# Where six chunks of x sums wait for their split, and which engine splits them

## The chip, the cores and the metric

The kernel runs on one core of a Trainium2 chip. The metric is the device time of one execution in microseconds (us), from the first to the last instruction and the little that lies around them; each version is run several times and the median counts. A core has a matrix engine (PE), a vector engine (DVE), an activation engine (ACT), GpSimd (POOL) and a sync engine (SP). Each takes its own instructions strictly in the order in which they were recorded. SP issues nearly all DMA transfers, ACT a few.

## What is computed

x has 2048 tokens of 576 features, all in float32:

```python
g = sigmoid((x * gate_w).sum(-1, keepdims=True))
a = linear_attention(x, wqkv, wo)                        # 32 heads of 18 features
b = (gelu(x @ w_gate) * (x @ w_up)) @ w_down             # 4608 hidden features
out = g * a + (1 - g) * b
```

## The kernel before

**Stages.** First come keys, values and their sums, then the queries and the attention's output, which is written to memory (`ga_d`) with the gate applied; then the gate and up products of `b`; then the down product, which adds all up. The change lies where the second stage ends and the third begins, between 260 and 310 us of the span.

**Numbers in two halves.** PE multiplies float32 in a rounded format (fp32r). So each operand is split: ACT copies it rounded into a high half, and DVE or POOL subtracts that copy from the raw value for the low half. One product of 128 x 512 results over half the features is then seven matmuls: six for the high and low halves of two blocks of 128 features, and one for the last 32 features.

**Gate and up.** A product of x and a weight block is done by Strassen's scheme: seven products of sums of blocks, numbered 1 to 7 in `PRODUCTS`, instead of eight. The seven operands that x gives are slots: `A11`, `A12` and `A22` (plain blocks) and the sums `S2`, `S4`, `S3`, `S1`. `xo` holds the seven slots of the first token half, `X[1]` (named `xo2` or `xo_3273`) those of the second. A weight block is loaded raw (`wraw`, in `stage`), POOL makes four differences of its blocks (`weight_sums`, L380), and `w_split` splits the seven operands into `W[GATE]` (`wg`) or `W[UP]` (`wu`): ACT L875, then POOL L876 and L877.

**Chains, frames, places.** One weight block on one token half is a chain of seven products; there are 72. A frame c has seven places i = 0 to 6: places 0, 4 and 5 run products 1, 6 and 2 of chain c, and places 1, 2, 3 and 6 run products 7, 5, 3 and 4 of chain c-1. Behind the product of a place, whatever `put` has entered in `plan[(frame, i)]` is recorded: loads, splits, sums, stores. Chain 0 is an exception: its first four products stand in the stage before, its fifth and sixth in frame 0, its seventh at place 1 of frame 1. Product 6 adds onto what product 1 left (a seed: ACT L948 or L950 copies one bank of results on; for the first chains DVE L956 then adds it), and products 2, 3 and 4 go on in the banks of 1, 6 and 7. So product 2 of chain 1 starts when ACT L948 has read the bank of product 1, and product 3 when another L948 has read the bank of product 6, once L956 has added to it. Product 4 follows DVE L983, which follows ACT L978 (the copy of product 5). DVE L922 and ACT L885 finish chain 0.

**The six chunks.** The sums S of the second token half are made early by POOL and stored to memory as `xsum_d[0..5]`, 512 KB each: chunk k has feature block k // 2 and 256 of the 512 token columns. `s_load(k)` (L1290, on SP) brings a chunk raw into one half of `f`, a buffer that later takes results of the second token half; `s_make(k)` splits it into `X[1]` (ACT L1295, then L1296, on DVE for chunks 0 to 3 and on POOL for 4 and 5). Chunks 0 and 1 are loaded ahead of frame 0 and chunk k + 2 right behind the split of k. The slots A11, A12 and A22 of `X[1]` are loaded ready-made from `xop_d` (L1363) at the places `X_AT`.

**Around it.** `w_fetch(1, 0)` (L865) loads the raw weights of chain 2, and L1324 those of chain 3. The last two stores of the attention's output (L797, issued by ACT from the buffer `ga`) are still under way here. `X[1]`, `f` and `stage` are new tiles which lie in memory that the stage before has used, so their first writer waits for the last user of what lay there.

Of the kernel before, what the change touches and what calls it, by code (L numbers as in the profile page):

```python
# [11 lines left out]
OP = mybir.AluOpType  # L12
# [102 lines left out]
A11, A12, A22, S2, S4, S3, S1 = range(7)  # L115
# [5 lines left out]
def tile_gated_mix(ctx, tc, xt, xs, xn, wk, wv, wq, wo, wgu, wdn, cst, out):  # L121
    nc = tc.nc
# [9 lines left out]
    xsum_d = [dram.tile([128, 4, 256], F32, name=f"xsum_d{k}") for k in range(6)]  # L132
# [8 lines left out]
    def f32(ap):  # L141
        return ap.bitcast(F32)
# [233 lines left out]
    def weight_sums(raw, out, parts=slice(0, 4)):  # L376
        b12, b11, b21, b22 = (raw[:, i] for i in range(4))
        t1, t2, t3, t4 = (out[:, i] for i in range(4))
        for o, a, b in ((t1, b12, b11), (t2, b22, t1), (t3, b22, b12), (t4, b21, t2))[parts]:
            nc.gpsimd.tensor_tensor(o, a, b, OP.subtract)  # L380
# [468 lines left out]
    X, ES = {0: xo}, {0: es}  # L849
# [14 lines left out]
    def w_fetch(n, m):  # L864
        nc.sync.dma_start(wraw, wgu[n, m])  # L865
        if (n, m) == (1, 1):
            nc.sync.dma_start(tsum, ws_d)
        else:
            weight_sums(wraw, tsum)
# [267 lines left out]
    f = stages.tile([128, 4, BS], F32, name="f")  # L1137
# [142 lines left out]
                h_load()  # L1280

    X_AT = {(0, 5): A11, (3, 4): A12, (4, 0): A22}
    S_AT = [(1, 1), (1, 4), (2, 1), (2, 5), (3, 1), (3, 3)]

    def s_raw(k):
        return f[:, k % 2 * 2:k % 2 * 2 + 2].rearrange("p a (b c) -> p (a b) c", b=2)

    def s_load(k):
        if k < 6:
            nc.sync.dma_start(s_raw(k), xsum_d[k])  # L1290

    def s_make(k):
        kt, c, raw = k // 2, slice(k % 2 * 256, k % 2 * 256 + 256), s_raw(k)
        rows, lo, eng = (slice(0, 128), 3 + kt, nc.vector) if kt < 2 else (slice(32, 64), kt, nc.gpsimd)
        nc.scalar.activation(X[1][:, S2:S1 + 1, kt, c], raw, AF.Copy)  # L1295
        eng.tensor_tensor(X[1][rows, S2:S1 + 1, lo, c], raw[rows], f32(X[1][rows, S2:S1 + 1, kt, c]), OP.subtract)  # L1296

    for k in range(2):
        s_load(k)
    w_fetch(1, 0)  # L1300
    LAST = len(CHAINS) - 1
    plan = {}

    def put(frame, i, do):
        plan.setdefault((frame, i), []).append(do)
# [45 lines left out]
    for g in range(NF2 // 2):  # L1351
        one = Sums(g)
        for at, what in one.tasks():
            frame, i = light[31 * g + at * 31 // 25]
            eng = nc.gpsimd if i > 3 or frame % 2 == 0 == i else nc.vector
            put(frame, i, lambda one=one, what=what, eng=eng: one.do(what, eng))
    for n, k in enumerate((1, 6, 2, 7, 5, 3, 4)):
        b = PRODUCTS[k][1]
# [2 lines left out]
            lambda b=b: nc.sync.dma_start(f32(last_up[:, b]), wp_d[1][:, b]))  # L1361
    for (frame, i), a in X_AT.items():
        put(frame, i, lambda a=a: nc.sync.dma_start(f32(X[1][:, a]), xop_d[:, a]))  # L1363
    for k, (frame, i) in enumerate(S_AT):
        put(frame, i, lambda k=k: s_make(k))
        put(frame, i, lambda k=k: s_load(k + 2))
    kept = [(0, es[1], (2, 4), (LAST, 1)), (1, sx[:, 0], (2, 4), (LAST, 1)), (2, es[2], (2, 6), (LAST, 3))]
    for c in range(1, LAST):
        for (frame, i), does in sorted(extras(c).items()):
            for do in does:  # L1370
                put(c + frame, i, do)
    late = extras(LAST)
    for do in late.pop(0):
        put(LAST, 4, do)
# [176 lines left out]
```

## Time and profile before

| | |
|---|---|
| median of 3 runs | 1445.23 us (1443.6 to 1445.69) |
| the profiled execution | 1443.79 us, span 1442.0 us, granted PE clock 1.000 |
| PE busy | 1435.1 us, in 8096 matmuls |
| DVE, ACT, POOL busy | 995.8, 640.5, 824.4 us |
| DMA | 312.69 MB, mean 217 GB/s |

In a timeline row stand the start and the length in us, the engine (SPq and ACTq are the issue of a DMA, not its transfer), the line of the code, the operation, output<-inputs, the shape, how many instructions the row merges, and in brackets how long the engine idled before it and what ended that. A matmul of a stream is shown with 0.39 us, though the next starts after 0.227 us: the ends are modelled and overlap. In a row of time windows stand the window, the busy us of each engine, the granted clock, the mean busy share of the 16 DMA engines and the GB/s (1 GB/s is 1 KB per us) that they moved.

### The profile page before, as it was taken

What the parts mean: (1) busy time and instruction counts of PE and PEld (TensorE: products, weight loads), DVE (VectorE), ACT (ScalarE), POOL (GpSimd) and SP (SyncE); (2) the same over time, 40 slices, a digit from 0 to 9 for tenths busy, and PEclk for the clock granted to TensorE, in tenths of its full rate; (3) what the DMA queues carried; (4) which work ended last, traced back from release to release, by engine and by line L of the source; (5) the groups of instructions that cost most, each with busy time, mean ns of one, the idle gap of its engine ahead of it and who ended that gap; (6) DMA issues with size and microseconds to landing.
All of it is one profiled execution on the core that took longest, in us unless ns stands there. A gap on an engine that the chain in (4) does not pass through costs nothing. (4 is left out here: it accounts for less than half of the span.)

```text
span 1442.0 us, 21510 instructions
## 1 busy us (share of the span) xinstructions
PE 1435.1 (100%) x8096; PEld 1281.3 (89%) x8096; DVE 995.8 (69%) x1139; ACT 640.5 (44%) x863; POOL 824.4 (57%) x541
## 2 busy tenths in 40 slices
PE   9999999999999999999999999999999999999999
PEld 9999899978888888888888888888889999999998
DVE  7887898355865648646485554766578777799793
ACT  7554656444333433334433344333355455444542
POOL 1674543366555655655556455564236565589895
PEclk9999999999999999999999999999999999999999
DMA  7573485774654556454664555655799989866761
GB/s 260 154 216 112 163 281 184 248 272 153 219 184 163 178 189 227 168 174 166 206 223 156 188 175 169 231 172 186 271 368 336 354 294 355 321 219 249 241 214 34
DMA packets 148552, 312.69 MB, mean 217 GB/s; under 512 B 14744, under 2 KB 61528, under 8 KB 147296
## 3 DMA queue, kind: packets, MB, share of 16 engines
q1 hardware_dynamic: 145856, 306.34, 62.1%
q10 hardware_dynamic: 2592, 4.98, 0.9%
q8 instruction: 63, 1.03, 0.3%
q14 instruction: 41, 0.34, 0.1%
HBM read 200.78 MB, written 110.44 MB: 216 GB/s over the span
## 5 line engine op out<-in xcount | busy, mean ns | idle before, releaser
L861 PE MATMUL bank<-xo,wg 128*128 128x512 f32 x1764 | 415.4, 389 | 0.3 <-ACT bank L950 0.2
L861 PE MATMUL bank<-xo,wu 128*128 128x512 f32 x1715 | 403.5, 389 | 0.3 <-ACT bank L950 0.3
L861 PEld LDWEIGHTS bank<-xo,wg 128*128 128x128 f32 x1764 | 330.9, 188 | 69.4 <-ACT bank L950 0.7
L861 PEld LDWEIGHTS bank<-xo,wu 128*128 128x128 f32 x1715 | 321.9, 188 | 67.5 <-ACT bank L950 0.8
L1437 PE MATMUL bank<-xo 128*128 128x288 f32 x2124 | 283.7, 294 | 0.7 <-DVE acc L1447 0.7
L1437 PEld LDWEIGHTS bank<-xo 128*128 128x128 f32 x2124 | 281.4, 188 | 1.1 <-DVE acc L1447 1.0
L380 POOL TENSOR_TENSOR stage<-stage 128x384 f32<-128x384 f32 x132 | 139.6, 1078 | 173.8 <-DMA stage<-wgu 144.0
L950 ACT ACTIVATE bank<-bank 128x512 f32<-128x512 f32 x139 | 80.9, 582 | 238.3 <-PE bank L861 230.1
L1240 POOL TENSOR_TENSOR xo<-vt,xo 128x864 fp32r<-128x864 f32 x39 | 112.7, 2892 | 51.5 <-ACT xo L1239 48.7
L1240 POOL TENSOR_TENSOR xo<-stage,xo 128x864 fp32r<-128x864 f32 x33 | 93.8, 2843 | 82.9 <-ACT xo L1239 57.0
L876 POOL TENSOR_TENSOR wg<-stage,wg 128x768 fp32r<-128x768 f32 (+3 forms) x41 | 73.8, 1801 | 87.9 <-ACT wg L875 84.1
L983 DVE TENSOR_TENSOR bank<-bank,mid 128x512 f32<-128x512 f32 x36 | 25.1, 697 | 133.4 <-ACT mid L978 133.4
L876 POOL TENSOR_TENSOR wu<-stage,wu 128x768 fp32r<-128x768 f32 (+2 forms) x36 | 75.1, 2087 | 62.6 <-ACT wu L875 56.3
L1437 PE MATMUL bank<-xo,wu 128*128 128x288 f32 x684 | 93.3, 294 | 0.0
L1437 PEld LDWEIGHTS bank<-xo,wu 128*128 128x128 f32 x684 | 91.3, 188 | 0.0
L978 ACT ACTIVATE mid<-bank 128x512 f32<-128x512 f32 x71 | 42.4, 597 | 102.2 <-PE bank L861 94.0
L980 DVE TENSOR_TENSOR f<-bank,mid 128x512 f32<-128x512 f32 x18 | 12.4, 692 | 96.8 <-ACT mid L978 93.0
L788 PEld LDWEIGHTS pair<-kw,p 128*128 128x128 f32 x448 | 60.8, 189 | 1.0
L788 PE MATMUL pair<-kw,p 128*128 128x288 f32 x448 | 61.4, 295 | 0.0
L538 PE MATMUL bank<-xo,qw 128*128 128x512 f32 (+1 forms) x231 | 55.7, 392 | 0.0
L538 PEld LDWEIGHTS bank<-xo,qw 128*128 128x128 f32 (+1 forms) x231 | 41.9, 183 | 10.0
L313 POOL TENSOR_TENSOR psum_k<-psum_k,e 128x576 f32<-128x576 f32 x14 | 20.6, 1470 | 50.0 <-DVE gate L306 48.5
(274 smaller groups left out, 2239.0 us busy)
## 6 DMA issues: line engine op xcount, KB each, us to landing
stage<-wgu SPq DMA_DIRECT2D x33, 768.0 KB, 5.4
wg<-h_d SPq DMA_DIRECT2D x28, 768.0 KB, 4.3
h_d<-sx SPq DMA_DIRECT2D x72, 256.0 KB, 2.1
hr<-h_d SPq DMA_DIRECT2D x24, 768.0 KB, 4.3
h_d<-mid SPq DMA_DIRECT2D x64, 256.0 KB, 4.3
h_d<-e SPq DMA_DIRECT2D x63, 256.0 KB, 3.9
xo<-h_d SPq DMA_DIRECT2D x17, 768.0 KB, 8.7
stage<-wdn SPq DMA_DIRECT2D x72, 144.0 KB, 3.4
```

Source lines behind the costliest of these rows:

```text
L313: (nc.vector if t < 2 else nc.gpsimd).tensor_tensor(psum_k, psum_k, r, OP.add)
L380: nc.gpsimd.tensor_tensor(o, a, b, OP.subtract)
L538: nc.tensor.matmul(ps[:wa.shape[1]], wa, xa, start=(k == 0), stop=(k == len(ops) - 1), skip_group_check=g == 4)
L788: nc.tensor.matmul(y[:, i, :288], p[:, 5 * a + g], KW[g][:, wl, i * 288:(i + 1) * 288], start=(n == 0), stop=(n == 13))
L861: nc.tensor.matmul(ps, w_, x_, start=start and i == 0, stop=i == 6, skip_group_check=not start)
L876: nc.gpsimd.tensor_tensor(w[:, i, 3:5], src[:, :, 0:2], f32(w[:, i, 0:2]), OP.subtract)
L950: nc.scalar.activation(o, src, AF.Copy)
L978: nc.scalar.activation(d_sum, d, AF.Copy)
L980: nc.vector.tensor_tensor(es[3], ps["c"], d_sum, OP.add)
L983: nc.vector.tensor_tensor(d, ps["c"], d_sum, OP.add)
L1240: nc.gpsimd.tensor_tensor(w[:, 1], src, f32(w[:, 0]), OP.subtract)
L1437: nc.tensor.matmul(y, h[:, hl, g, t * 128:(t + 1) * 128], w[:, wl, g * 288:(g + 1) * 288], start=first and c == 0 and n == 0, stop=c == NK ...
```

## The change

All six chunks are loaded ahead of frame 0. Chunks 2 and 3 go raw into the slot A12 of `X[1]`, chunks 4 and 5 into A22, which both get their own content later; 0 and 1 go into `f` as before. The loads of 2 to 5 are issued ahead of the weights of chain 2, those of 0 and 1 behind them. The splits come in the order 2, 3, 4, 5, 0, 1, in frames 0 to 2 instead of 1 to 3, all low halves on DVE. And one sum of results, DVE's L1003 of chain 1, moves from place 3 to place 4 of frame 2, behind product 6.

```diff
-    S_AT = [(1, 1), (1, 4), (2, 1), (2, 5), (3, 1), (3, 3)]
+    S_AT = {(0, 5): 2, (0, 6): 3, (1, 0): 4, (1, 1): 5, (1, 4): 0, (2, 1): 1}

     def s_raw(k):
-        return f[:, k % 2 * 2:k % 2 * 2 + 2].rearrange("p a (b c) -> p (a b) c", b=2)
+        room = f if k < 2 else f32(X[1][:, A12 if k < 4 else A22])
+        return room[:, k % 2 * 2:k % 2 * 2 + 2].rearrange("p a (b c) -> p (a b) c", b=2)
...
-        rows, lo, eng = (slice(0, 128), 3 + kt, nc.vector) if kt < 2 else (slice(32, 64), kt, nc.gpsimd)
+        rows, lo = (slice(0, 128), 3 + kt) if kt < 2 else (slice(32, 64), kt)
         nc.scalar.activation(X[1][:, S2:S1 + 1, kt, c], raw, AF.Copy)
-        eng.tensor_tensor(X[1][rows, S2:S1 + 1, lo, c], raw[rows], f32(X[1][rows, S2:S1 + 1, kt, c]), OP.subtract)
-
+        nc.vector.tensor_tensor(X[1][rows, S2:S1 + 1, lo, c], raw[rows], f32(X[1][rows, S2:S1 + 1, kt, c]), OP.subtract)
+
+    for k in range(2, 6):
+        s_load(k)
+    w_fetch(1, 0)
     for k in range(2):
         s_load(k)
-    w_fetch(1, 0)
...
-    for k, (frame, i) in enumerate(S_AT):
+    for (frame, i), k in S_AT.items():
         put(frame, i, lambda k=k: s_make(k))
-        put(frame, i, lambda k=k: s_load(k + 2))
...
-                put(c + frame, i, do)
+                put(c + frame, i + ((c, frame, i) == (1, 1, 3)), do)
```

On SP, right behind the last weights of chain 1 (L839), there stood (in brackets the semaphores that a row waits for; `xsum_d_73` to `xsum_d_78` are chunks 0 to 5):

```order
L1290 DMA f<-xsum_d_73 128x1024 [waits DMAHW2_49,PE_49,Activation_49]
L1290 DMA f<-xsum_d_74 128x1024 [waits DMAHW4_49]
L865 DMA stage<-wgu 128x1536 [waits DMAHW5_49,DVE_49,Activation_49]
L1324 DMA stage<-wgu 128x1152 [waits DMAHW6_49]
L1363 DMA xo_3273<-xop_d 128x2560 [waits DMAHW1_49,DMAHW3_49,DMAHW0_49,DMAHW7_49,Activation_49,Pool_49]
```

and now:

```order
L1290 DMA xo_3273<-xsum_d_75 128x1024 [waits DMAHW1_49,DMAHW2_49,DMAHW0_49,DMAHW3_49,DVE_49,DMAHW6_49,Activation_49,Pool_49]
L1290 DMA xo_3273<-xsum_d_76 128x1024 [waits DMAHW4_49]
L1290 DMA xo_3273<-xsum_d_77 128x1024 [waits DMAHW5_49]
L1290 DMA xo_3273<-xsum_d_78 128x1024
L865 DMA stage<-wgu 128x1536 [waits DMAHW7_49]
L1290 DMA f<-xsum_d_73 128x1024
L1290 DMA f<-xsum_d_74 128x1024
L1326 DMA stage<-wgu 128x1152
L1365 DMA xo_3273<-xop_d 128x2560 [waits DMAHW3_49]
```

The first write to `X[1]`, with its waits for the last users of that memory, was the load of A11 (L1363), behind both weight loads; now it is the load of chunk 2, ahead of them. In the built program the counts that it waits for on DMAHW1, DMAHW2 and DMAHW0 are those of the last three stores of `ga` (L797), the same three that L1363 waited for; the latest is the store issued last.

On ACT, from the first split of chain 2's weights (L875, which reads what L865 loads), there stood

```order
L875 ACTIVATE wg<-stage 128x2x384
L885 ACTIVATE e_3265<-e_3265 128x512
L948 ACTIVATE sx<-bank 128x512
L875 ACTIVATE wg<-stage 128x2x384
L885 ACTIVATE e_3265<-e_3265 128x512
L875 ACTIVATE wg<-stage 128x384 x3
L1295 ACTIVATE xo_3273<-f 128x4x256
L948 ACTIVATE sx<-bank 128x512
```

and now

```order
L875 ACTIVATE wg<-stage 128x2x384
L885 ACTIVATE e_3265<-e_3265 128x512
L1295 ACTIVATE xo_3273<-xo_3273 128x4x256 x2
L948 ACTIVATE sx<-bank 128x512
L875 ACTIVATE wg<-stage 128x2x384
L1295 ACTIVATE xo_3273<-xo_3273 128x4x256
L885 ACTIVATE e_3265<-e_3265 128x512
L875 ACTIVATE wg<-stage 128x384 x3
L1295 ACTIVATE xo_3273<-xo_3273 128x4x256
L948 ACTIVATE sx<-bank 128x512
```

Two splits now stand ahead of the first L948, and two more, instead of one, between it and the second.

On DVE the piece of the difference from the last sums of chain 0 (L910, L916, L922) on is

```order
 L910 TENSOR_TENSOR e_3265<-bank,mid 128x512
 L916 TENSOR_TENSOR e_3265<-bank,mid 128x512
+L1296 TENSOR_TENSOR xo_3273<-xo_3273 128x4x256 x2
+L1296 TENSOR_TENSOR xo_3273<-xo_3273 32x4x256
 L922 TENSOR_TENSOR e_3265<-bank,mid 128x512
-L1296 TENSOR_TENSOR xo_3273<-f,xo_3273 128x4x256
+L1296 TENSOR_TENSOR xo_3273<-xo_3273 32x4x256
 L956 TENSOR_TENSOR bank<-bank,sx 128x512
 L1296 TENSOR_TENSOR xo_3273<-f,xo_3273 128x4x256
```

Ahead of L922 stand three subtractions where none stood, and each of them waits for the L1295 of its chunk; between L922 and the first L956 one stands as before.

More of the change, by code (lines that the diff above doesn't have):

```diff
@@ L1282, in tile_gated_mix @@
     X_AT = {(0, 5): A11, (3, 4): A12, (4, 0): A22}
-    S_AT = [(1, 1), (1, 4), (2, 1), (2, 5), (3, 1), (3, 3)]
+    S_AT = {(0, 5): 2, (0, 6): 3, (1, 0): 4, (1, 1): 5, (1, 4): 0, (2, 1): 1}
     def s_raw(k):
-        return f[:, k % 2 * 2:k % 2 * 2 + 2].rearrange("p a (b c) -> p (a b) c", b=2)
+        room = f if k < 2 else f32(X[1][:, A12 if k < 4 else A22])
+        return room[:, k % 2 * 2:k % 2 * 2 + 2].rearrange("p a (b c) -> p (a b) c", b=2)
     def s_load(k):
-        if k < 6:
-            nc.sync.dma_start(s_raw(k), xsum_d[k])
+        nc.sync.dma_start(s_raw(k), xsum_d[k])
     def s_make(k):
         kt, c, raw = k // 2, slice(k % 2 * 256, k % 2 * 256 + 256), s_raw(k)
-        rows, lo, eng = (slice(0, 128), 3 + kt, nc.vector) if kt < 2 else (slice(32, 64), kt, nc.gpsimd)
+        rows, lo = (slice(0, 128), 3 + kt) if kt < 2 else (slice(32, 64), kt)
         nc.scalar.activation(X[1][:, S2:S1 + 1, kt, c], raw, AF.Copy)
-        eng.tensor_tensor(X[1][rows, S2:S1 + 1, lo, c], raw[rows], f32(X[1][rows, S2:S1 + 1, kt, c]), OP.subtract)
+        nc.vector.tensor_tensor(X[1][rows, S2:S1 + 1, lo, c], raw[rows], f32(X[1][rows, S2:S1 + 1, kt, c]), OP.subtract)
+    for k in range(2, 6):
+        s_load(k)
+    w_fetch(1, 0)
     for k in range(2):
         s_load(k)
-    w_fetch(1, 0)
     LAST = len(CHAINS) - 1
```

## The prediction

> **What bounds the kernel.** I read the page's engine table first, then PE's waits around the change, then the timeline there.
>
> ```profile
> PE 1435.1 (100%) x8096; PEld 1281.3 (89%) x8096; DVE 995.8 (69%) x1139; ACT 640.5 (44%) x863; POOL 824.4 (57%) x541
> ```
>
> PE is busy for 1435.1 of 1442.0 us, so nothing but a PE wait taken away or added moves the end: the change can win what PE idles near it, and lose without limit. PE's own waits between 270 and 312 us come to one row:
>
> ```profile
> PE bank L861 <- ACT bank L950: 0.6, 2, 0.3
> ```
>
> Both places in the timeline, with the rows that end them:
>
> ```profile
> 291.32 3.33 PE L861 MATMUL bank<-xo,wu 128*128 128x512 f32 x14
> 292.93 0.69 DVE L1003 TENSOR_TENSOR sx<-mid,e 128x512 f32<-128x512 f32 x1
> 293.54 0.69 DVE L956 TENSOR_TENSOR bank<-bank,sx 128x512 f32<-128x512 f32 x1
> 294.26 0.58 ACT L950 ACTIVATE bank<-bank 128x512 f32<-128x512 f32 x1 [5.21 <-DVE bank L956]
> 294.90 5.08 PE L861 MATMUL bank<-xo,wg 128*128 128x512 f32 x21 [0.24 <-ACT bank L950]
> ...
> 302.99 3.33 PE L861 MATMUL bank<-xo,wg 128*128 128x512 f32 x14
> 305.06 1.06 ACT L1295 ACTIVATE xo<-f 128x1024 fp32r<-128x1024 f32 x1 [1.18 <-DMA f<-xsum_d]
> 306.03 0.58 ACT L950 ACTIVATE bank<-bank 128x512 f32<-128x512 f32 x1
> 306.66 5.06 PE L861 MATMUL bank<-xo,wu 128*128 128x512 f32 x21 [0.34 <-ACT bank L950]
> ```
>
> A stream's matmuls start 0.227 us apart (below), so 14 from 291.32 let the next start at 294.50; it started at 294.90. Likewise 306.17 against 306.66. PE loses 0.40 + 0.49 = 0.9 us here. The first wait is an L956 behind a sum (L1003) on DVE, the second a split (L1295) that waited for its chunk.
>
> **What goes.** The moved sum lets that L956 start 0.6 us sooner, which covers 0.40; with no split left in frame 3 the second wait loses its cause. Gain: up to 0.9 us. POOL loses two subtractions; nobody waits for POOL there, so that is worth nothing.
>
> **What comes: the order of loads.** These rows are DMA issues and the first readers of chain 2's weights:
>
> ```profile
> 267.99 0.80 SPq L1290 DMA_DIRECT2D f<-xsum_d  x2
> 268.90 0.40 SPq L865 DMA_DIRECT2D stage<-wgu  x1
> 271.66 0.33 ACTq L797 DMA_DIRECT2D ga_d<-ga  x1
> 275.33 0.83 ACT L875 ACTIVATE wg<-stage 128x768 fp32r<-128x768 f32 x1
> 275.45 4.06 POOL L380 TENSOR_TENSOR stage<-stage 128x384 f32<-128x384 f32 x4 [27.19 <-ACT e L885]
> 277.69 0.33 SPq L1363 DMA_DIRECT2D xo<-xop_d  x1
> ```
>
> L1363 stood on SP from about 270 to 277.69, since its slot lies over `ga` and the last L797 store (issued 271.66) had to land. That cost nothing, as only A11 was behind it. Now that wait stands at the head, ahead of L865. The weights of chain 2 landed by 275.4 (POOL's start, put down to an L885 that it doesn't need).
>
> When will the store land with nothing else in flight? The windows:
>
> ```profile
> 265.50:266.50 1.00, 1.00 (x10) 1.00 (x9) 0.00 (x0) 0.00 (x0) 0.00 (x0) 1.00 0.77 295
> 268.00:270.00 2.00, 2.00 (x17) 2.00 (x16) 0.00 (x0) 0.00 (x0) 0.00 (x0) 1.00 0.52 124
> 270.00:277.00 7.00, 7.00 (x35) 5.95 (x34) 2.08 (x3) 2.74 (x4) 1.47 (x2) 1.00 1.01 394
> 277.00:278.00 1.00, 1.00 (x6) 0.81 (x6) 0.00 (x0) 0.61 (x2) 1.00 (x2) 1.00 0.04 12
> 280.00:282.40 2.40, 2.40 (x12) 2.01 (x11) 0.00 (x0) 2.38 (x5) 2.24 (x3) 1.00 0.99 418
> ```
>
> An earlier store of `ga` and the one landing that the trace has for line L797:
>
> ```profile
> 264.82 0.33 ACTq L797 DMA_DIRECT2D ga_d<-ga  x1
> ```
> ```profile
> DMA to landing us min/median/max: 3.3/3.3/3.3
> ```
>
> The earlier store was issued at 264.82 the queues empty and had moved its 295 KB by 266.50, 1.7 us later; and SP went on 0.65 us after the bytes stopped at about 277.05. That gives 2.3 us; the landing is 3.3 us. So SP's first load goes at 274.0 to 275.0 instead of 267.99; I take 274.4.
>
> When will the weights land? From the first issue at 267.99, two us brought 248 KB, and then 394 KB per us flowed. Ahead of and with L865 there are now four chunks (2097 KB) and 786 KB of weights: 2.0 + (2883 - 248) / 394 = 8.7 us, or 8.1 at the 418 to 430 of a load alone (last window). I take 8.5: W = 282.9, bounds 282.1 to 283.7, where W was 275.4. Four issues of 0.40 (L865's row) stay ahead of the data.
>
> **The chain behind W.** L875 heads ACT's queue until W, and everything behind it waits. The rows for the steps:
>
> ```profile
> 274.79 0.63 ACT L885 ACTIVATE e<-e 128x512 f32<-128x512 f32 x1 [3.16 <-DVE e L910]
> 280.09 1.34 ACT L875 ACTIVATE wg<-stage 128x384 fp32r<-128x384 f32 x3
> 279.47 1.29 POOL L876 TENSOR_TENSOR wg<-stage,wg 128x512 fp32r<-128x512 f32 x1
> 281.33 1.04 ACT L1295 ACTIVATE xo<-f 128x1024 fp32r<-128x1024 f32 x1
> 284.67 0.60 ACT L948 ACTIVATE sx<-bank 128x512 f32<-128x512 f32 x1 [2.30 <-DVE bank L956]
> 278.83 0.69 DVE L922 TENSOR_TENSOR e<-bank,mid 128x512 f32<-128x512 f32 x1 [2.48 <-PE bank L861]
> 283.95 0.69 DVE L956 TENSOR_TENSOR bank<-bank,sx 128x512 f32<-128x512 f32 x1
> L1296 DVE TENSOR_TENSOR xo<-f,xo x4: 1208/1395/1644, 282.5 to 298.2; 128x1024 fp32r<-128x1024 f32 x4
> 278.62 3.34 PE L861 MATMUL bank<-xo,wu 128*128 128x512 f32 x14
> 281.80 1.75 PE L861 MATMUL bank<-xo,wg 128*128 128x512 f32 x7
> ```
>
> PE's 14 matmuls of products 6 and 2 of chain 1 take 281.80 - 278.62, 0.227 each: product 2 was due at 280.2. Neighbours on ACT overlap by 0.09 (274.79 + 0.63 against 275.33); I take off 0.08 for each.
>
> First wait: L875 0.83, L885 0.63, two L1295 of 1.04, L948 0.60, less overlaps, and 0.05 to PE (294.84 to 294.90 in the first place above): W + 3.9 = 286.8 instead of 280.2, **6.6 us**. POOL's part (four L380, then chain 2's first low halves) falls within the second wait.
>
> Second wait: ACT's second L875 and third L1295 end at W + 5.65. DVE's subtraction of chunk 4, with 32 rows, is not in the trace; by the 128-row form it is 1.2 to 1.64, and I take the median 1.4, as length along the row is equal: W + 7.05. L922 to 7.7, L885 8.35, three L875 9.6, L1295 10.6, subtraction 12.05, L956 12.7, L948 13.3, PE at W + 13.35. Product 3 is due 28 matmuls after product 2, at W + 10.25: **3.1 us** (2.7 to 3.6).
>
> Third: behind that L948, L1295, subtraction, L943, L956, subtraction and L983 (0.96 + 1.4 + 3 x 0.65 + 1.4 + 0.65 less overlaps) end 5.65 later, and product 4 is due 21 matmuls or 4.75 after product 3: **0.9 us** (0.6 to 1.3). The weights of chain 3 hang on DVE and POOL rows that move along with these, so I add nothing for them.
>
> On the subtractions the Trainium skill, SBUF — State Buffer, section "SBUF: two separate sides", says that DVE and GpSimd hold one pair of ports in turn, and the later one is blocked for the whole instruction. By it a subtraction behind a fresh POOL L876 of 1.29 us could take 1.2 + 1.3 = 2.5, an estimate, and the second wait 5.3. The trace has 1.64 as the longest of the four, though POOL worked beside it, so I stay with the median.
>
> **Sum.** 6.6 + 3.1 + 0.9 - 0.9 = +9.7 us, or 1453.5 against the profiled execution's 1443.79. That lies 1.44 under the median of the runs; I add half of it: 1454.2. Own range: lowest ends 5.8 + 2.7 + 0.6 - 0.9 = +8.2, highest 7.4 + 3.6 + 1.3 = +12.3, so 1452 to 1457.5 with the median's uncertainty.
>
> **Rivals.**
> *The load order costs, the SP wait doesn't* (SP goes at 267.99 as before). For: the L797 store might land sooner than I think. Against: L1363's 277.69. Then W is later only by 1049 KB / 394 = 2.7, at 278.1: 1.8 + 3.1 + 0.9 - 0.9 = +4.9, 1449.4 with that share of the median.
>
> *Not slower.* The slots are free before `f`, so that the four chunks land while SP used to wait:
>
> ```profile
> L1290 SPq EVENT_SEMAPHORE  x5: 17/17/6681, 261.3 to 296.4; - x5
> ```
>
> SP stood idle for 6.68 us from 261.3 to 268, enough for 2 MB. L875 then starts at 275.33, L948 ends at 279.5 in time, but the same steps from there bring PE to product 3 at 288.9, due at 286.55: 2.35, and 0.9 behind it, less 0.9: 1446.8 with the median's share, within 0.2% (2.9 us, about what a measurement of this kernel tells from no change). The point that decides is a W below 276. Against: the list of waits is that of L1363.
>
> *A slow PE after the wait.* PE has rows at another pace:
>
> ```profile
> 1.20:4.70 3.50, 3.50 (x16) 3.50 (x17) 1.17 (x4) 2.33 (x5) 0.00 (x0) 1.00 0.84 234
> ```
>
> and its longest wait is that of the span's start:
>
> ```profile
> PE kpair L216 <- DVE zeros L210: 1.2, 1, 1.2
> ```
>
> Its first 16 matmuls of 256 columns took 0.219 each, where 512 columns take 0.227 later: half speed for 3.5 us after rest (the granted clock column reads 1.00 all the same). No wait is over 1.2 us, so whether 6.6 us bring it back is open. If so, 8 to 16 matmuls lose 0.21 each, 1.7 to 3.3; the second wait's 3.1 hides that unless the slow spell falls behind it. Then about +2.5: 1456.7. The Trainium skill, TensorE: Matmul & The Clock Gate, section "What's actually happening", has this rule: about 3.4 us idle halve the clock, and as long a busy window restores it. By it the first wait is enough; the first rows agree.
>
> **How the numbers follow.** Forecast 0.76, load order alone 0.08, slow PE 0.09, not slower 0.07. The range 1450.0 to 1458.0 holds the first and third and leaves out the others. Slower 0.92; of the last case 0.06 is no change and 0.02 faster, since only 0.9 us can be won here.
>
> **What would show it.** SP's first L1290 near 274.4; L875 and L380 starting near 282.9; PE waiting for L948 twice (6.6, 3.1), then for L983; no PE wait for L950 over 0.2. Chunks landed before 276 or a PE that never waits for L948 would prove me wrong.

## The result, and the profile after

The change makes the kernel slower: a median of 1456.03 us (1455.61 to 1456.62, 6 runs) against 1445.45 (1443.6 to 1446.38, 6 runs) of before; the ratio is 1.0076, with an interval of 1.0065 to 1.0087. 1454.2 was predicted, with a range of 1450 to 1458. The profiled execution took 1456.62 us, its span 1454.8.

From the page of the kernel after, the line of engines:

```profile
PE 1438.9 (99%) x8096; PEld 1284.0 (88%) x8096; DVE 997.8 (69%) x1141; ACT 640.0 (44%) x863; POOL 821.6 (56%) x539
```

From its list of PE's waits over the whole span (total, times, longest):

```profile
PE bank L861 <- ACT sx L948: 9.2, 2, 7.5
```

No wait for L948 stood there before. The waits for L950, 0.6 us between 270 and 312 us before, are gone from the list. And PE is busy 3.8 us longer with as many matmuls: some of them ran slower.

From its timeline, the rows behind both waits. Clocks of two traces differ: the first matmul of frame 0 stands at 270.27 here and at 270.69 before, so 0.42 must be added here to compare with rows of before.

```profile
270.27 4.92 PE L861 MATMUL bank<-xo,wg 128*128 128x512 f32 x21
271.24 0.33 ACTq L797 DMA_DIRECT2D ga_d<-ga  x1
273.53 1.75 SPq L1290 DMA_DIRECT2D xo<-xsum_d  x4
275.32 0.50 SPq L865 DMA_DIRECT2D stage<-wgu  x1
...
283.68 0.84 ACT L875 ACTIVATE wg<-stage 128x768 fp32r<-128x768 f32 x1 [8.68 <-DMA stage<-wgu]
286.02 6.08 DVE L1296 TENSOR_TENSOR xo<-xo 128x1024 fp32r<-128x1024 f32 x3 [10.10 <-ACT xo L1295]
286.84 0.58 ACT L948 ACTIVATE sx<-bank 128x512 f32<-128x512 f32 x1
287.47 3.35 PE L861 MATMUL bank<-xo,wu 128*128 128x512 f32 x7 [7.52 <-ACT sx L948]
288.05 1.05 ACT L1295 ACTIVATE xo<-xo 128x1024 fp32r<-128x1024 f32 x1
288.76 2.26 POOL L876 TENSOR_TENSOR wg<-stage,wg 128x512 fp32r<-128x512 f32 x1
290.62 2.82 PE L861 MATMUL bank<-xo,wg 128*128 128x512 f32 x7
293.28 3.37 PE L861 MATMUL bank<-xo,wu 128*128 128x512 f32 x14
...
298.34 1.89 PE L861 MATMUL bank<-xo,wu 128*128 128x512 f32 x7 [1.69 <-ACT sx L948]
303.94 3.48 PE L861 MATMUL bank<-xo,wu 128*128 128x512 f32 x14 [0.54 <-DVE bank L983]
...
323.22 3.11 PE L861 MATMUL bank<-xo,wg 128*128 128x512 f32 x13
```

SP's first chunk load goes 2.3 us after the last store of `ga` was issued; the chunk loads and L865 leave without a pause; 10.15 us after the first issue the weights are there, and L875, which heads ACT's queue, starts. L948 follows two splits later and PE 0.05 behind it.

From its windows (columns as before: PE, PEld, DVE, ACT, POOL busy, granted clock, DMA share, GB/s):

```profile
280.00:282.00 2.00, 0.00 (x0) 0.00 (x0) 0.00 (x0) 0.00 (x0) 0.00 (x0) 1.00 1.02 418
282.00:284.00 2.00, 0.00 (x0) 0.00 (x0) 0.00 (x0) 0.32 (x1) 0.19 (x1) 0.66 1.01 414
284.00:286.00 2.00, 0.00 (x0) 0.00 (x0) 0.00 (x0) 2.00 (x4) 1.92 (x3) 0.50 1.03 420
...
290.00:292.00 2.00, 2.00 (x6) 1.49 (x6) 2.00 (x1) 0.00 (x0) 1.92 (x2) 0.50 0.00 0
292.00:294.00 2.00, 2.00 (x9) 1.58 (x8) 0.79 (x2) 1.15 (x3) 1.92 (x2) 0.78 0.00 0
```

From 280 to 283.7 us every engine is idle and only DMA works: that is the price of the load order. The granted clock falls to 0.50 while PE waits (at about 282.6, read in windows of 0.25 us), and stays there until about 292.9, 5.4 us after PE has gone on at 287.47: 6 matmuls in 2 us, where the full clock makes 9.

**Where the time went.** From the first matmul of frame 0 to a matmul 175 further on, which both kernels reach with the same work done, 175 x 0.2268 = 39.7 us are needed (0.2268 us from one matmul's start to the next is the pace of the run `behind` below, which never waits here). Before took 40.87 (270.69 to 311.56, the rows below), after 52.95 (270.27 to 323.22): 12.1 us more.

```profile
270.69 4.92 PE L861 MATMUL bank<-xo,wg 128*128 128x512 f32 x21
...
311.56 0.62 PE L861 MATMUL bank<-xo,wg 128*128 128x512 f32 x2
```

They are:

- 7.7 us at product 2 of chain 1, due at 279.8 (42 matmuls behind 270.27) and started at 287.47;
- 4.5 us up to product 3. Its 28 matmuls ahead need 6.36 us and the start came 10.87 later. The profile shows 1.7 of it as a wait; the other 2.8 are matmuls at half clock, which make the wait look shorter and cost nothing of their own (the run `warm` below);
- 0.83 us at product 4, and 0.2 in remnants, less the 1.17 that before lost there.

The two profiled executions differ by 12.8 us, the medians by 10.6; the 0.7 in the remaining stages of the profiled execution was not traced to the change.

### The profile page after: what moved, and what is told of

It is laid out like the page before. It is cut to its first block, busy times and chain, and to the rows that moved or that the text cites. A ratio compares the mean times of both kernels' runs of the same rounds, so it can differ in the third digit from the quotient of the medians.

```text
span 1454.8 us, 21500 instructions
## 1 busy us (share of the span) xinstructions
PE 1438.9 (99%) x8096; PEld 1284.0 (88%) x8096; DVE 997.8 (69%) x1141; ACT 640.0 (44%) x863; POOL 821.6 (56%) x539
## 5 line engine op out<-in xcount | busy, mean ns | idle before, releaser
L380 POOL TENSOR_TENSOR stage<-stage 128x384 f32<-128x384 f32 x132 | 140.8, 1088 | 180.7 <-DMA stage<-wgu 178.1
L950 ACT ACTIVATE bank<-bank 128x512 f32<-128x512 f32 x139 | 80.9, 582 | 239.3 <-PE bank L861 234.2
L876 POOL TENSOR_TENSOR wg<-stage,wg 128x768 fp32r<-128x768 f32 (+3 forms) x41 | 74.8, 1824 | 94.9 <-ACT wg L875 91.7
L983 DVE TENSOR_TENSOR bank<-bank,mid 128x512 f32<-128x512 f32 x36 | 25.1, 696 | 133.7 <-ACT mid L978 133.7
L876 POOL TENSOR_TENSOR wu<-stage,wu 128x768 fp32r<-128x768 f32 (+2 forms) x36 | 74.1, 2058 | 63.0 <-ACT wu L875 56.5
L978 ACT ACTIVATE mid<-bank 128x512 f32<-128x512 f32 x71 | 42.5, 599 | 101.6 <-PE bank L861 93.4
L980 DVE TENSOR_TENSOR f<-bank,mid 128x512 f32<-128x512 f32 x18 | 12.5, 692 | 97.5 <-ACT mid L978 97.5
L877 POOL TENSOR_TENSOR wg<-stage,wg 32x384 fp32r<-32x384 f32 (+3 forms) x41 | 47.5, 1157 | 3.2
```

The costliest lines, as they stand in the source:

```text
L876: nc.gpsimd.tensor_tensor(w[:, i, 3:5], src[:, :, 0:2], f32(w[:, i, 0:2]), OP.subtract)
L877: nc.gpsimd.tensor_tensor(w[64:96, i, 2], src[64:96, :, 2], f32(w[64:96, i, 2]), OP.subtract)
L950: nc.scalar.activation(o, src, AF.Copy)
L978: nc.scalar.activation(d_sum, d, AF.Copy)
L980: nc.vector.tensor_tensor(es[3], ps["c"], d_sum, OP.add)
L983: nc.vector.tensor_tensor(d, ps["c"], d_sum, OP.add)
```

## The experiments

Two theories stood against each other. *Head of the queue:* the cost is the order of the loads, the wait for the stores of `ga` first, then four chunks ahead of the weights; everything behind L875 slides. *Order of the splits:* the early splits on ACT and DVE cost by themselves, with the weights in time. A third point was whether PE's half clock costs anything.

**wfirst: the weights first, all else as after.**

```diff
+    w_fetch(1, 0)
     for k in range(2, 6):
         s_load(k)
-    w_fetch(1, 0)
```

> The changed kernel with one move: the weights of chain 2 (L865) are issued ahead of all six chunks. Theory (weights that land 8 us late make the first PE wait, the new order of splits the rest): L875 starts near 275 again, the first wait of PE for L948 (7.5 us) and the drop of the PE clock vanish; product 3 of chain 1 still waits for the second L948, 2.4 to 3.7 us, and product 4 for L983, 0.5 to 0.9: 1447.5 to 1449.5 us. Rival 1 (the order of the splits alone makes the loss): still near 1456. Rival 2 (the order of the loads is all of it): 1444.5 to 1445.5.

Measured: 1449.81 us (1447.35 to 1449.98, 6 runs) against 1444.81, ratio 1.0029 (1.0017 to 1.0041): +5.0. From its timeline:

```profile
265.27 0.34 SPq L865 DMA_DIRECT2D stage<-wgu  x1
269.61 4.06 POOL L380 TENSOR_TENSOR stage<-stage 128x384 f32<-128x384 f32 x4 [21.52 <-DMA stage<-wgu]
273.98 1.75 SPq L1290 DMA_DIRECT2D xo<-xsum_d  x4
275.33 0.83 ACT L875 ACTIVATE wg<-stage 128x768 fp32r<-128x768 f32 x1
278.83 2.36 DVE L1296 TENSOR_TENSOR xo<-xo 128x1024 fp32r<-128x1024 f32 x2 [2.48 <-DMA xo<-xsum_d]
290.13 2.66 PE L861 MATMUL bank<-xo,wu 128*128 128x512 f32 x7 [3.05 <-ACT sx L948]
...
296.63 3.33 PE L861 MATMUL bank<-xo,wu 128*128 128x512 f32 x14
```

The chunk loads wait at the same place as in after (273.98), but harm nothing in front of them: the weights have landed by 269.61, when POOL's L380 starts on them, L875 starts at 275.33, behind an L885, and the first wait is gone. The second stays, 3.05 us with the weights in time. So both theories hold for a part. The wait for L983 that was expected did not come, and the drop of the clock that was to vanish did: the result lies 0.3 above the expected span, because the clock halved behind the 3.05 us of waiting, where nothing hides it:

```profile
292.00:294.00 2.00, 2.00 (x6) 1.52 (x6) 2.00 (x4) 1.67 (x3) 1.55 (x2) 0.50 0.17 57
```

21 matmuls from 290.13 took 6.5 us instead of 4.8. The one run of six whose clock averaged 1.000 instead of 0.999 took 1447.35.

**loadsonly: after's loads, before's places, order and engines of the splits (the moved sum stays).**

```diff
-    S_AT = {(0, 5): 2, (0, 6): 3, (1, 0): 4, (1, 1): 5, (1, 4): 0, (2, 1): 1}
+    S_AT = {(1, 1): 0, (1, 4): 1, (2, 1): 2, (2, 5): 3, (3, 1): 4, (3, 3): 5}
...
-        rows, lo = (slice(0, 128), 3 + kt) if kt < 2 else (slice(32, 64), kt)
+        rows, lo, eng = (slice(0, 128), 3 + kt, nc.vector) if kt < 2 else (slice(32, 64), kt, nc.gpsimd)
...
-        nc.vector.tensor_tensor(X[1][rows, S2:S1 + 1, lo, c], raw[rows], f32(X[1][rows, S2:S1 + 1, kt, c]), OP.subtract)
+        eng.tensor_tensor(X[1][rows, S2:S1 + 1, lo, c], raw[rows], f32(X[1][rows, S2:S1 + 1, kt, c]), OP.subtract)
```

> The changed order of loads alone: chunks 2 to 5 raw in the slots and ahead of the weights, but the splits at the places, in the order and on the engines of before (the moved sum stays moved). Theory (the late weights cost by themselves): L875 starts near 283.7; the first wait ends with the low halves of chain 2's weights on GpSimd, 7 to 7.5 us; the clock drops, and its 28 slow matmuls are no longer hidden by a second wait: 1452 to 1456 us, 1455 if the half clock costs in full, 1452 if not. Rival (the loss needs the new order of the splits): under 1449.

Measured: 1452.44 us (1451.38 to 1452.53, 4 runs), ratio 1.0052 (1.0036 to 1.0069): +7.6. From its timeline:

```profile
283.50 0.84 ACT L875 ACTIVATE wg<-stage 128x768 fp32r<-128x768 f32 x1 [8.04 <-DMA stage<-wgu]
285.40 3.27 PE L861 MATMUL bank<-xo,wu 128*128 128x512 f32 x7 [4.99 <-ACT sx L948]
288.51 1.85 PE L861 MATMUL bank<-xo,wg 128*128 128x512 f32 x7
290.20 5.14 PE L861 MATMUL bank<-xo,wu 128*128 128x512 f32 x21
```

The weights are nearly as late as in after (L875 starts 12.8 us behind the first matmul of frame 0, there 13.4), and PE goes on 1.9 us after L875 instead of 3.8, since no split stands between. 5.0 us of waiting remain, and 1.6 of half clock (14 matmuls in 4.8 us instead of 3.2), uncovered here too. The wait for POOL's L876 that was expected did not come. Loads alone cost 7.6 and the new splits without late weights (wfirst) 5.0; together they cost 10.6, less than the sum: each alone also pays 1.6 to 1.7 us for slow matmuls, which the pair hides in its second wait.

**onechunk: one chunk ahead of the weights instead of four.**

```diff
-    for k in range(2, 6):
-        s_load(k)
+    s_load(2)
     w_fetch(1, 0)
-    for k in range(2):
+    for k in (3, 4, 5, 0, 1):
         s_load(k)
```

> The changed kernel with the weights of chain 2 issued behind the first chunk instead of the fourth: the wait for the stores of ga stays ahead of them, three chunks (1573 KB) less do. Theory (the wait and the queue each cost their part): SP goes at 274, the weights land at 279 to 280 instead of 283.7, the first wait of PE for L948 shrinks from 7.5 to 3 to 4 us; 1451 to 1453.5 us. Rival (the wait at the head is nearly all, since the transfers overlap anyway): 1455 to 1456. Rival (the wait costs nothing, only the bytes ahead do): no first wait, as with the weights ahead of all chunks: 1449 to 1450.

Measured: 1451.87 us (1451.2 to 1454.55, 4 runs) against 1444.61, ratio 1.0052 (1.0039 to 1.0066). From its timeline:

```profile
274.30 0.42 SPq L865 DMA_DIRECT2D stage<-wgu  x1
279.39 0.85 ACT L875 ACTIVATE wg<-stage 128x768 fp32r<-128x768 f32 x1 [4.00 <-DMA stage<-wgu]
```

SP's wait stays (the first load goes at 273.93). Counted from the first matmul of frame 0, L875 starts after 4.6 us in wfirst, 8.7 here and 13.4 in after: the late start and one chunk move it by 4.1 us (in wfirst it waited for ACT's L885, not for the weights), the other three chunks by 4.7, or 4.0 with the 12.8 of loadsonly. Of the time, 7.3 us are lost all the same, because here the waits stand apart (2.8 for L948, 1.3 and 0.5 for POOL) and are followed by a slow spell.

**pool45: the low halves of chunks 4 and 5 on POOL again.**

```diff
-        rows, lo = (slice(0, 128), 3 + kt) if kt < 2 else (slice(32, 64), kt)
+        rows, lo, eng = (slice(0, 128), 3 + kt, nc.vector) if kt < 2 else (slice(32, 64), kt, nc.gpsimd)
...
-        nc.vector.tensor_tensor(X[1][rows, S2:S1 + 1, lo, c], raw[rows], f32(X[1][rows, S2:S1 + 1, kt, c]), OP.subtract)
+        eng.tensor_tensor(X[1][rows, S2:S1 + 1, lo, c], raw[rows], f32(X[1][rows, S2:S1 + 1, kt, c]), OP.subtract)
```

> The changed kernel with the low halves of chunks 4 and 5 on GpSimd as before, all else as changed. Theory (three subtractions ahead of L922 on VectorE set the second wait): L922 and the second L948 come at least 2 us sooner, the second wait (1.7 us) goes, and PE at half clock is then the bound there: 1454 to 1455 us. Rival (what the second wait waits for is ScalarE's queue, not VectorE): no change, 1456. Rival (GpSimd's two subtractions of 2.4 us make the weights of chain 3 late): a new wait of PE at product 1 of chain 3, 1456 or more.

Measured: 1458.93 us (1458.41 to 1459.54, 4 runs), ratio 1.0097 (1.0082 to 1.0112). From its timeline:

```profile
292.21 4.93 PE L861 MATMUL bank<-xo,wu 128*128 128x512 f32 x21
...
302.33 2.35 POOL L1296 TENSOR_TENSOR xo<-xo 32x1024 fp32r<-32x1024 f32 x1
304.76 1.59 POOL L1321 TENSOR_TENSOR wu<-stage,wu 128x512 fp32r<-128x512 f32 x1
306.40 1.94 PE L861 MATMUL bank<-xo,wu 128*128 128x512 f32 x5 [3.62 <-POOL wu L1321]
```

With two subtractions fewer on DVE the second wait is gone: product 3, the last seven of the 21 matmuls from 292.21, starts at 295.4 without one. POOL, which is behind with the weights already, takes the subtractions and is late with those of chain 3: 3.6 us of a new wait. So the expected 1454 to 1455 was missed, and the rival of late weights for chain 3 held. DVE was the right place, given the late weights.

**warm: PE kept busy.** Product 6 of chain 1 runs five times instead of once, so that PE has work during the wait.

```diff
-            product(p, k, w, o, fresh)
+            for _ in range(5 if (c, name) == (1, "b") else 1):
+                product(p, k, w, o, fresh)
```

> The changed kernel, in which PE runs product 6 of chain 1 five times into the same bank with the same result: 28 matmuls or 6.4 us more, all within the first wait of 7.5 us. Theory (the half clock after the wait is hidden under the second wait): the granted clock stays at 1.0, products 2, 1, 7 and 5 run at 0.227 us a matmul, and the second wait for L948 grows from 1.7 to 4.0 to 4.6 us; the time stays within 0.5 us of the changed kernel, 1455.5 to 1456.5. Rival (the half clock costs what it takes, 28 matmuls with 2.8 us more): 1453 to 1453.5.

Measured: 1456.9 us (1456.61 to 1457.58, 4 runs), ratio 1.0084 (1.0069 to 1.0099), not to be told from after's 1.0076. From its timeline and its windows:

```profile
298.65 3.21 PE L861 MATMUL bank<-xo,wu 128*128 128x512 f32 x7 [1.89 <-ACT sx L948]
```
```profile
300.00:302.00 2.00, 2.00 (x6) 1.61 (x5) 2.00 (x4) 2.00 (x4) 1.92 (x2) 0.50 0.00 0
```

The seven matmuls behind the first wait (1.2 us now) follow at 0.25 us each, not 0.45, and product 3 still starts at 298.65, 14.7 us behind the weights (L875 at 283.96), as in after (14.66): ACT and DVE set that moment, not PE. That settles the disputed cost: in after, the half clock costs nothing up to product 3. The expectation that the clock would stay at 1.00 failed: it fell later, after waits of 1.2, 1.3, 0.5 and 1.9 us within 12 us. There the slow matmuls are not hidden: product 4 starts at 305.15, 34.6 us behind the first matmul of frame 0 against 33.7 in after, and the median lies 0.4 us above the expected span.

**behind: raw loads that nobody waits behind.** Chunks 0 and 1 into `f`, then the weights of chain 2 and 3, then A11 as before; chunks 2 to 5 go raw into their slots behind that, at place 0 of frame 1; splits as before, the sum moved.

```diff
-    S_AT = {(0, 5): 2, (0, 6): 3, (1, 0): 4, (1, 1): 5, (1, 4): 0, (2, 1): 1}
+    S_AT = {(1, 1): 0, (1, 4): 1, (2, 1): 2, (2, 5): 3, (3, 1): 4, (3, 3): 5}
...   (the low halves of chunks 4 and 5 on POOL, as in loadsonly)
-    for k in range(2, 6):
-        s_load(k)
-    w_fetch(1, 0)
     for k in range(2):
         s_load(k)
+    w_fetch(1, 0)
...
+    for k in range(2, 6):
+        put(1, 0, lambda k=k: s_load(k))
```

> What is worth keeping: weights of chain 2 ahead of every load into the slots, the four chunks loaded behind those weights and behind the load of A11 (place 0 of frame 1), the splits at the places, in the order and on the engines of before, the moved sum kept. Theory: no PE wait between 270 and 312 us, both small ones of before (0.40 and 0.49 us) gone, L875 near 275.3: 0.9 us less than before, 1443.5 to 1445 in the time, which alone can't tell it from before. Rival (the four chunk loads delay a later load that PE needs): a new wait, 1446 or more.

Measured: 1443.28 us (1442.45 to 1444.27, 11 runs) against 1444.61 (21 runs), ratio 0.9991 (0.9983 to 1.0). From its timeline:

```profile
271.03 4.92 PE L861 MATMUL bank<-xo,wg 128*128 128x512 f32 x21
...
278.32 0.33 SPq L1363 DMA_DIRECT2D xo<-xop_d  x1
278.70 2.34 SPq L1290 DMA_DIRECT2D xo<-xsum_d  x4
...
310.73 1.52 PE L861 MATMUL bank<-xo,wg 128*128 128x512 f32 x6
```

SP waits for the stores as long as ever, ahead of A11, which nobody needs yet. PE goes from 271.03 to 310.73 in 39.70 us: nothing is lost. The trace shows the whole 1.17 us that before lost regained; the runs agree with it in size (1.3), but their interval ends at 1.0, and it is within the 0.2% that counts as no change. It is the best version found.

**sumonly: before, with the moved sum alone.**

```diff
-                put(c + frame, i, do)
+                put(c + frame, i + ((c, frame, i) == (1, 1, 3)), do)
```

> The kernel before with the moved sum alone. Theory: the PE wait of 0.24 us for L950 at 294.9 goes, the other of 0.34 us stays; 0.4 us less, not to be told from before by time: 1443.5 to 1446. Rival (another row on VectorE holds L956): the wait stays.

Measured: 1444.16 us (1442.19 to 1446.05, 10 runs), ratio 0.9998 (0.9988 to 1.0007): no change. Both waits for L950, 0.24 and 0.34 us, are gone from the list (the second was expected to stay), but the same stretch of PE's work takes 41.03 us (270.49 to 311.52), no less than before. From its timeline:

```profile
301.09 1.06 ACT L1295 ACTIVATE xo<-f 128x1024 fp32r<-128x1024 f32 x1 [0.49 <-DMA f<-xsum_d]
302.06 0.58 ACT L978 ACTIVATE mid<-bank 128x512 f32<-128x512 f32 x1
302.67 0.69 DVE L980 TENSOR_TENSOR e<-bank,mid 128x512 f32<-128x512 f32 x1 [1.65 <-ACT mid L978]
303.42 3.51 PE L861 MATMUL bank<-xo,wg 128*128 128x512 f32 x14
```

PE was due at 302.99, and each row ends where the next begins: the split that waited for its chunk now holds up L978, L980 and a product. The losses moved; as long as a split waits for its load, ACT's queue waits with it. In behind, where the raw chunks lie ready and the sum is moved too, they are gone.

## Why the prediction was right, and where its sizes were off

- **SP's wait at the head: right.** The first load went at 273.95 on before's clock, at the low end of the stated 274.0 to 275.0; 274.4 was taken.
- **Landing of the weights, W: 1.2 us too early.** 284.1 on before's clock against 282.9 and an upper bound of 283.7. The step that failed is the sum of the bytes due up to the weights: the queue took 10.15 us, not 8.5. The packets of the trace tell why in part. A row of these weights is one packet of 6144 bytes, a row of a chunk one of 4096. The last of the 128 weight packets ended at 283.23; by then 574 chunk packets had ended, 62 more than the four chunks ahead of the weights have. So 254 KB of a later load arrived before the last weights, 0.65 us at 394 KB per us. And L875 started 0.45 us after that last packet; before, too, POOL started 0.47 us after it (274.98 and 275.45). The sum has neither term: it counts only the bytes ahead, and ends with the last of them. Why later packets came first is not shown.
- **First wait: right in its chain** (W + 3.8, predicted W + 3.9); 7.7 us instead of 6.6, all through W, and beyond its stated 5.8 to 7.4.
- **Second wait: 4.5 us instead of 3.1** (2.7 to 3.6 stated), by one term: a DVE subtraction of 1.4 us, from the median before. Three took 6.08, or 2.03 each, beside POOL's back-to-back work. That moved the path, too: the prediction waited for ACT's third split, done at W + 5.65, and one subtraction behind it, W + 7.05. The split was done at W + 5.4 (288.05 and 1.05), but DVE was still at the first two, and its third ended at W + 8.4. In wfirst two with POOL idle took 2.36, or 1.18 each. How the two engines hold each other up is seen where they meet singly, in after's timeline:

```profile
295.71 1.22 DVE L1296 TENSOR_TENSOR xo<-xo 32x1024 fp32r<-32x1024 f32 x1 [2.89 <-ACT xo L1295]
295.78 1.46 POOL L877 TENSOR_TENSOR wg<-stage,wg 32x128 fp32r<-32x128 f32 x1
...
298.12 0.45 POOL L877 TENSOR_TENSOR wg<-stage,wg 32x128 fp32r<-32x128 f32 x1
...
300.89 1.30 POOL L1321 TENSOR_TENSOR wu<-stage,wu 128x512 fp32r<-128x512 f32 x1
...
301.61 1.67 DVE L1296 TENSOR_TENSOR xo<-f,xo 128x1024 fp32r<-128x1024 f32 x1
```

  At 295.71 DVE started first and took its 1.22; the L877 of POOL behind it took 1.46 instead of 0.45, and ended about 0.3 us after DVE. At 301.61 POOL was already at work, until 302.19; there DVE took 1.67. The section of the Trainium skill that was weighed (SBUF — State Buffer, "SBUF: two separate sides") says that whichever starts first holds the ports for its whole instruction, and the other is blocked. These rows agree, and the 2.5 us worked out by it was nearer to 2.03 than the median was.
- **Third wait: right,** 0.83 us against 0.9. **The gain: right,** the waits for L950 and 1.0 of the 1.17 us are gone. `sumonly` shows that the moved sum alone does not bring it, `behind` that the sum and the early raw chunks together do; early chunks without the moved sum were not run.
- **The slow PE: happened, and cost nothing here.** The prediction named the condition: the second wait hides it unless it falls behind. It fell inside, and `warm` shows it.
- **"Load order without the SP wait" and "not slower" fell** with L1290 at 273.53 and `onechunk`.

The sum was 9.7 us in the profile and 12.1 were measured there: 1.1 from W and 1.4 from the subtraction, less 0.1. Between the medians it was 10.6, and that the measured time lies near the 1456.7 of the slow PE is chance: the excess came from W and the subtraction. Some slips in the working moved nothing of weight: ACT's second L875 and third L1295 end at about W + 5.55 by its own rows, not 5.65, its bracket for the third wait counts one 0.65 more than the chain that it lists (the 5.65 goes with the list), and the shares of the last case add up to 0.08, not 0.07.

## What to carry to other kernels

A new tile's first writer takes over the wait for whatever lay in that memory; before a load is moved to the head of a queue, look at what its destination waits for and at who stands behind it, and leave it behind what is needed first. Here a raw buffer that is free early was worth having only for loads that nobody queues behind: `behind` has the same buffers as the change and loses nothing. Price an operation of an engine by the state of its neighbour at the new place, not by its median at the old one.

## What the runs showed of the hardware

- PE's granted clock fell to 0.50 about 2.7 us into an idle stretch and returned 5.4 us after work resumed (after: idle from 279.95, 282.6, 287.47, 292.9). In other runs it fell when PE was already at work again: 0.9 us after a single wait of 3.05 us (wfirst), 0.2 us after the last of four waits of at most 1.9 us within 12 us (warm), and 0.35 us after waits of 1.3 and 0.5 us (onechunk), where PE had idled 1.7 of the 3.4 us ahead of the fall. Each slow spell is a whole multiple of 3.41 us: 3.41 in wfirst, loadsonly, onechunk and warm, 6.83 and 3.41 in pool45, 10.24 in after. The Trainium skill, TensorE: Matmul & The Clock Gate, section "What's actually happening", gives an idle window of about 3.4 us for the drop and a busy one as long for the return, both free-running. The multiples agree with such a window; that it has to be idle throughout is not what onechunk shows.
- A subtraction over 32 partitions takes as long as over 128 of the same length: 1.22 us at 295.71 in after, where it started ahead of POOL, against 1.18 in wfirst with POOL idle.
